# A transformer block with segment memory on one core: attention scheduled among the projections, V as the stationary operand, FFN in two token blocks

## Chip, cores, metric

One core of a Trainium2 chip. The metric is device time in microseconds (us) of one execution.

## The reference

One sequence of 2048 tokens, width 1024, bf16. A pre-norm block: attention in four segments with a compressive memory that is carried from segment to segment, then a gated FFN of width 3584. Cut to what is computed:

```python
def _A_ref(x, wq, wk, wv, wo, beta):            # x: layernorm of A_x, [1, 2048, 1024]
    q, k, v = x @ wq, x @ wk, x @ wv             # 32 heads of 32, 4 segments of 512 tokens
    phi = lambda t: where(t > 0, t + 1.0, exp(t))
    g = sigmoid(beta)                            # one gate a head
    M, z = 0, 0                                  # memory of a head: 32 x 32, and 32
    for s in range(4):
        p = softmax(qs @ ks.T * 32**-0.5 + causal mask)
        a_dot = p @ vs
        a_mem = (phi(qs) @ M) / (phi(qs) @ z + 1e-06)
        o = g * a_mem + (1.0 - g) * a_dot
        M, z = M + phi(ks).T @ vs, z + phi(ks).sum(l)
    return o @ wo
h  = A_x + _A_ref(layernorm(A_x), ...)
h2 = h + (silu(ln @ w1) * (ln @ w3)) @ w2        # ln = layernorm(h); F = 3584
```

In matmuls of 128 x 128 weights against 512 columns the dense part is 768 for q, k and v, 256 for the output projection, 1792 for w1 and w3 and 896 for w2: 3712 in all.

## The kernel before

Five phases run one after the other, with a wait of every engine for every other between them (`sync_all`). Inside each phase the order is written out by hand, and every engine executes its own instructions in that order.

**Phase AB** (`phase_AB`): the layer norm of 16 token tiles (statistics L317 and L320, square root on ACT L151, apply L324), transposes on PE (L343) and copies on ACT (L352), then per 512 tokens the projections (L383) on four PSUM banks, copied out by DVE (L392) and ACT (L395, L406). All of q, k (transposed, `qT`, `kT`) and v (`vaug`, with a 33rd column per head) stay in SBUF.

**Phase C** (`phase_C`): 8 groups of 4 heads, 4 segments each, so 32 steps, pipelined by one: the head of a step between the tail pieces of the step before. The head makes the scores of four key tiles (`head_kc`; L580, four matmuls side by side, one for each head's 32 rows), each followed by one exponential on ACT over four banks (L589) and the triangle mask on DVE (L603). The tail multiplies by V (L631): a 128 x 128 block of exponentials is the stationary operand and 33 columns of V move through, so 1280 matmuls of 33 columns in all; then it reads the memory (L677, 384 matmuls of 33 columns), divides and adds on DVE (L700 to L709), and updates the memory (L648 to L752). phi is computed for a whole group at a time (`group_prep`, L548 to L555).

**Phase D** (`phase_D`): per token tile, transposes of the attention output (L839), copies (L848, L853), the output projection (L869), residual add (L883), second layer norm (L896 to L903), transposes (L921) and copies (L928, L934).

**Phase F** (`phase_F`): 14 chunks of w1 and w3 (256 columns each), all 2048 tokens for each: gate (L1011), up (L1017), sigmoid on ACT (L1028), two products on DVE (L1033, L1038). **Phase G** (`phase_G`): four blocks of 512 tokens; w2 comes in 7 slices for every block (28 loads of 1 MB); the matmuls (L1098) fill eight banks, and at the end of a block eight residual adds (L1120) and eight stores follow.

## Time and profile before

| | |
|---|---|
| Time, median of 3 runs | 1230.05 us (1229.1 to 1231.36) |
| Span of the profiled execution | 1229.1 us; its own time is 1229.1 us too (the fastest of the three) |
| PE (matmul) busy | 981.4 us, 80% |
| DVE / ACT / POOL busy | 507.0 / 339.9 / 21.1 us |
| DMA traffic | 66.05 MB, mean 54 GB/s |

L1011 stands for line 1011 of the kernel. PE is TensorE, PEld its weight loads, DVE VectorE, ACT ScalarE, POOL GpSimd. PEclk is the granted clock of TensorE as a share of 2.4 GHz, so 0.50 is 1.2 GHz. A group's mean duration of a matmul contains its latency, and matmuls overlap: what one costs in a stream is read from the distance of the starts. An "idle before" names what ended an engine's wait.

### The profile page before, as it was taken

How to read it: one execution, taken by the hardware profiler on the slowest of the kernel's cores; microseconds unless marked ns; L12 is line 12 of the kernel's file. 1: busy time of each engine (PE TensorE's matmuls, PEld its weight loads, DVE VectorE, ACT ScalarE, POOL GpSimd, SP SyncE). 2: the span in 40 equal slices, each digit the busy share in tenths (PEclk: the TensorE clock that was granted, in tenths of full speed). 3: DMA queues.
4: the chain of work that ended last, by engine and by line, in shares of the span. 5: the costliest groups of instructions: out<-in, count | busy, mean ns of one | idle time of the engine just before them, and what ended most of it. 6: DMA issues, size and time to landing. Idle time of an engine off the chain costs nothing.

```text
span 1229.1 us, 16143 instructions
## 1 busy us (share of the span) xinstructions
PE 981.4 (80%) x6752; PEld 470.9 (38%) x6752; DVE 507.0 (41%) x1010; ACT 339.9 (28%) x423; POOL 21.1 (2%) x43
## 2 busy tenths in 40 slices
PE   4988989244444544578869999999999997999997
PEld 2434444132222322334424444444444443444443
DVE  5240310466666776657734333334444430101011
ACT  3224122565555665522211111111111110000000
POOL 1000000000000000000000000000000000001011
PEclk9999989555555555589989999999999998999999
DMA  8010000100000000011121111111111103555453
GB/s 307 1 35 1 1 1 1 69 2 1 1 1 1 2 1 1 1 44 52 43 69 35 36 35 35 35 53 50 35 36 35 35 1 107 176 164 201 139 189 120
DMA packets 54232, 66.05 MB, mean 54 GB/s; under 512 B 1936, under 2 KB 30608, under 8 KB 54160
## 3 DMA queue, kind: packets, MB, share of 16 engines
q1 hardware_dynamic: 52624, 60.83, 15.8%
q0 software_dynamic: 1536, 4.20, 0.9%
q8 instruction: 53, 0.87, 0.3%
q14 instruction: 19, 0.16, 0.0%
HBM read 60.83 MB, written 4.19 MB: 53 GB/s over the span
## 4 chain that ended last, share of the span: by engine, by line
PE 71%; ACT 16%; DVE 8%; DMA 2%; issue 2%; POOL 0%; SPq 0%; ACTq 0%; DVEq 0%; POOLq 0%
PE psall L1011 16%; PE psall L1017 16%; PE psall L1098 15%; PE psall L383 12%; ACT eTbuf L589 11%; PE psall L869 5%; PE psall L580 4%; ACT tmp L552 2%; ACT xnT L352 1%; DVE lnst L317 1%; DVE pkTg L555 1%; PE psall L631 1%; DMA w2b<-in_B_w_dram 1%; PE psall L921 1%; PE psall L648 1%
## 5 line engine op out<-in xcount | busy, mean ns | idle before, releaser
L1011 PE MATMUL psall<-hnT,w1b 128*128 128x512 bf16 x896 | 213.2, 381 | 6.8 <-DMA w3b<-in_B_w_dram 6.8
L1017 PE MATMUL psall<-hnT,w3b 128*128 128x512 bf16 x896 | 211.7, 379 | 0.0
L1098 PE MATMUL psall<-w2b,hmT 128*128 128x512 bf16 x896 | 195.3, 381 | 7.7 <-DMA w2b<-in_B_w_dram 7.7
L589 ACT ACTIVATE eTbuf<-psall 128x2048 bf16<-128x2048 f32 (+3 forms) x128 | 158.4, 1237 | 70.6 <-PE psall L580 69.9
L580 PE MATMUL psall<-qT,kT 32*128 32x256 bf16 (+3 forms) x512 | 58.0, 443 | 148.4 <-ACT eTbuf L589 142.8
L1033 DVE TENSOR_TENSOR sg<-sg,psall 128x512 bf16<-128x512 bf16 x112 | 77.1, 688 | 238.5 <-PE psall L1017 226.6
L1028 ACT ACTIVATE sg<-psall 128x512 bf16<-128x512 f32 x112 | 66.9, 597 | 315.6 <-PE psall L1011 315.6
L1098 PEld LDWEIGHTS psall<-w2b,hmT 128*128 128x128 bf16 x896 | 87.9, 98 | 115.2 <-issue 10.0
L1011 PEld LDWEIGHTS psall<-hnT,w1b 128*128 128x128 bf16 x896 | 87.9, 98 | 113.4 <-issue 8.6
L1017 PEld LDWEIGHTS psall<-hnT,w3b 128*128 128x128 bf16 x896 | 87.7, 98 | 105.9 <-issue 0.5
L1120 DVE TENSOR_TENSOR ob<-hnat,psall 128x512 bf16<-128x512 bf16 x32 | 22.0, 688 | 180.3 <-PE psall L1098 180.0
L1038 DVE TENSOR_TENSOR hmT<-sg,psall 128x512 bf16<-128x512 bf16 x112 | 76.9, 687 | 3.8
L580 PEld LDWEIGHTS psall<-qT,kT 32*128 32x128 bf16 x512 | 14.0, 99 | 164.2 <-ACT eTbuf L589 159.5
L869 PE MATMUL psall<-wosb,otT 128*128 128x512 bf16 x256 | 60.1, 389 | 16.0 <-ACT otT L853 16.0
L631 PE MATMUL psall<-vaug,eTbuf 128*128 128x33 bf16 x1280 | 53.8, 193 | 23.9 <-DVE onat L709 22.0
L383 PE MATMUL psall<-xnT,wq 128*128 128x512 bf16 x256 | 64.7, 418 | 9.3 <-ACT xnT L352 6.8
L603 DVE TENSOR_TENSOR eTbuf<-eTbuf,triu 128x512 bf16<-128x512 bf16 x128 | 54.4, 425 | 40.6 <-ACT eTbuf L589 30.4
L631 PEld LDWEIGHTS psall<-vaug,eTbuf 128*128 128x128 bf16 x1280 | 43.5, 107 | 56.3 <-DVE onat L709 33.2
L383 PE MATMUL psall<-xnT,wk 128*128 128x512 bf16 x256 | 55.9, 379 | 0.0
L383 PE MATMUL psall<-wv,xnT 128*128 128x512 bf16 x256 | 55.9, 379 | 0.0
L383 PEld LDWEIGHTS psall<-xnT,wq 128*128 128x128 bf16 x256 | 26.5, 105 | 46.4 <-issue 11.1
L392 DVE CAST qT<-psall 128x512 bf16<-128x512 f32 x32 | 21.3, 689 | 54.1 <-PE psall L383 54.1
(70 smaller groups left out, 596.0 us busy)
## 6 DMA issues: line engine op xcount, KB each, us to landing
w2b<-in_B_w_dram SPq DMA_DIRECT2D x28, 1024.0 KB, 5.3
w1b<-in_B_w_dram SPq DMA_DIRECT2D x14, 512.0 KB, 4.0
w3b<-in_B_w_dram SPq DMA_DIRECT2D x14, 512.0 KB, 5.4
xb<-in_A_x_dram SPq DMA_DIRECT2D x4, 1024.0 KB, 6.8
xr<-in_A_x_dram SPq DMA_DIRECT2D x16, 256.0 KB, 2.7
out_dram<-ob POOLq DMA_DIRECT2D x32, 128.0 KB, 2.4
wq<-in_A_wq_dram SPq DMA_DIRECT2D x1, 2048.0 KB, 12.8
wk<-in_A_wk_dram SPq DMA_DIRECT2D x1, 2048.0 KB, 17.7
```

The lines of the kernel that those rows point to most:

```text
L383: o = pe.matmul(self.bank(b), lhsT, rhs, start=(c == 0), stop=(c == NKC - 1))
L580: o = pe.matmul(self.bank(j, N), lhsT, rhs, start=True, stop=True, tile_position=(32 * j, 0))
L589: o = act.activation(eTbuf[:, :, offs[kc]:offs[kc] + N], src, AF.Exp, scale=scale)
L603: o = dve.tensor_tensor(eTbuf[:, :, offs[kc]:offs[kc] + 128], eTbuf[:, :, offs[kc]:offs[kc] + 128], self.triu[:, :].unsqueeze(1).to_broadc ...
L631: o = pe.matmul(self.ps_all[:, ucol(j, i):ucol(j, i) + 33], lhsT, rhs, start=(kc == 0), stop=(kc == i))
L869: o = pe.matmul(self.bank(bb + half), ob[:, c, :], self.wo_sb[:, c, half * 512:(half + 1) * 512], start=(c == 0), stop=(c == NKC - 1))
L1011: o = pe.matmul(self.bank(bg), w1b[i][:, c, jj * 128:(jj + 1) * 128], self.hnT[:, c, tc * 512:(tc + 1) * 512], start=(c == 0), stop=(c == ...
L1017: o = pe.matmul(self.bank(bu), w3b[i][:, c, jj * 128:(jj + 1) * 128], self.hnT[:, c, tc * 512:(tc + 1) * 512], start=(c == 0), stop=(c == ...
L1028: o = act.activation(sg[si][:, :], self.bank(bg), AF.Sigmoid)
L1033: o = dve.tensor_tensor(sg[si][:, :], sg[si][:, :], self.bank(bg), op=ALU.mult)
L1038: o = dve.tensor_tensor(self.hmT[:, fc, tc * 512:(tc + 1) * 512], sg[si][:, :], self.bank(bu), op=ALU.mult)
L1098: o = pe.matmul(self.bank(bb), self.hmT[:, fc, t * 128:(t + 1) * 128], w2b[k % 2][:, jj, half * 512:(half + 1) * 512], start=(fc == 0), st ...
```

## The change

The kernel is rewritten. All work is entered into a graph as operations with the engines that may run them, a cost in ns, a class (lower goes first), and the buffers they read and write. `schedule` then plays the graph through: whenever an engine is free it takes the ready operation of the lowest class whose PSUM banks are free, and its cost decides when its users become ready. The order that comes out for each engine is fixed in the program; on the chip an engine executes its list in that order, with semaphore waits. The costs are linear in the columns (`mm_ns`: n/2.4 + 2.6 ns for a matmul, `dve_ns`: 150 + n/0.96, `act_ns`: 185 + 0.834 n, `pool_ns`: 220 + 1.05 n), with a fixed latency to the user (260 ns behind PE, 110 to 130 behind the others) and 60 ns for a change of the PE's tiling.

What is computed by what:

- **Segments instead of phases.** Layer norm, q, k, v and memory of segment s+1 are entered ahead of the attention of segment s and share the engines with it, as does the output projection of the segment (`run`, below). Classes on PE: scores 0, PV 1, memory read 2, transposes of the norms 2 and 3, memory update 4, output projection 5, projections 6, FFN up 7, FFN down 8. wq, wk and wv come in halves of 1 MB, anew for every segment, into three buffers. q, k and v have two buffers each (even and odd segments).
- **PSUM.** Attention has banks 0 to 3 (scores), 4 and 5; everything dense has banks 6 and 7; only once the last score operation has started does the FFN get the other six as well.
- **Scores.** Three exponentials a step instead of four (the third and fourth key tile share one of 384 columns a head); the mask is an `affine_select` on POOL, 4 a step, instead of a product on DVE.
- **PV.** V (128 keys x 32) is the stationary operand, the exponentials move through, 512 to 128 columns, four heads side by side in column tiles; the output is transposed, so the transposes of phase D go. The row sums come from a second such pass with a matrix of one column of ones (`ones32`). The memory is read by two full matmuls a step. Division: 32 x 32 block transposes on DVE of the sums, a reciprocal, and block transposes that spread it again; the memory part is multiplied and added on POOL.
- **phi** is taken on 1024 columns at a time: exponential on ACT, minimum and maximum on DVE, the sum on POOL. The norm's square root is a power of -0.5 on POOL, the FFN's sigmoid a Tanh with the rest in DVE's products.
- **FFN.** Two blocks of 1024 tokens. `ffn_up` loads w1 and w3 in 14 chunks for each block (so twice in all); `ffn_down` keeps all 7 MB of w2 resident, works one half of a token tile after the other (28 matmuls into one bank), adds the residual, which was written to and read back from a DRAM scratch (`h_scr`), and stores. The buffer `hm` of the FFN's first block lies over q, k and v (its first 12 of 28 tiles over those of the even segments), w1 and w3 over the projections' weights and the normed input, w2 over attention buffers.
- All transfers are issued from the SP queue, in the planned order.

The core of the diff, new lines only (the old kernel goes entirely):

```diff
+    PAGE = 1024
+    LAT = {"pe": 260.0, "act": 110.0, "dve": 110.0, "pool": 130.0, "dma": 150.0}
+    SWITCH = 60.0
+    DMA_RATE = 260.0
+    DMA_FIX = 1900.0
...
+            moved = True
+            while moved:
+                moved = False
+                for e in ENGINES:
+                    if not free[e]:
+                        continue
+                    skipped = []
+                    pick = None
+                    while avail[e]:
+                        item = heapq.heappop(avail[e])
+                        o = item[2]
+                        if o in started:
+                            continue
+                        if not can_start(o):
+                            skipped.append(item)
+                            continue
+                        pick = o
+                        break
+                    for it in skipped:
+                        heapq.heappush(avail[e], it)
...
+def act_ns(n, ptr=0):
+    return 185.0 + n * 0.834 + 93.0 * ptr
+def dve_ns(n, mode=1):
+    return 150.0 + n / (0.96 * mode)
+def pool_ns(n):
+    return 220.0 + n * 1.05
+def mm_ns(n):
+    return max(n, 66) / 2.4 + 2.6
...
+    def dense_group(self, late=False):
+        g = Group([(6,), (7,)],
+                  ("att", [(4,), (5,), (0,), (1,), (2,), (3,)]) if late else None, True)
+        return g
...
+    def ln(self, k, src, dst, cls):
...
+        ve, rs = self.lnve[:, k:k + 1], self.rstd[:, k:k + 1]
+        var, mean = self.lnmv[:, k, 1:2], self.lnmv[:, k, 0:1]
+        mh = self.mhalf[:, :]
+        self.pool_op(lambda e: e.tensor_scalar(ve, var, self.EPS, None, op0=ALU.add), 1,
+                     [var], [ve], 0)
+        self.pool_op(lambda e: e.tensor_tensor(rs, ve, mh, op=ALU.pow), 300, [ve, mh], [rs], 0)
+        self.dve_op(lambda e: e.tensor_scalar(dst, src, mean, rs, op0=ALU.subtract,
+                                              op1=ALU.mult), 540.0, [src, mean, rs], [dst], cls)
...
+    def phi(self, src, dst, cls):
...
+        self.act(e_, src, AF.Exp, act_ns(1024), cls=cls)
+        self.dve_op(lambda e: e.tensor_scalar(e_, e_, 1.0, None, op0=ALU.min), dve_ns(1024, 4),
+                    [e_], [e_], cls)
+        self.dve_op(lambda e: e.tensor_scalar(r, src, 0.0, None, op0=ALU.max), dve_ns(1024, 4),
+                    [src], [r], cls)
+        self.pool_op(lambda e: e.tensor_tensor(dst, e_, r, op=ALU.add), 1024, [e_, r], [dst],
+                     cls)
...
+    def unit(self, s, g, q, k, v, pq):
+        G = self.g
+        u = self.n_unit % 2
+        self.n_unit += 1
+        e0, e1, e2 = self.e0[u], self.e1[u], self.e2[u]
+        pm = (s - 1) % 2
...
+        for batch in (0, 1, 2):
+            gr = self.queue(0, 1, 2, 3)
+            kcs = ((0,), (1,), (2, 3))[batch]
+            width = (512, 384, 384)[batch]
+            et = (e0, e1, e2)[batch]
+            def emit(e, gr, kcs=kcs):
+                ins = []
+                off = 0
+                for kc in kcs:
+                    n = 512 - 128 * kc
+                    for j in range(4):
+                        r = slice(32 * j, 32 * j + 32)
+                        ins.append(e.matmul(self.bank(gr, j, n, off),
+                                            k[r, g, 128 * kc:128 * kc + 128],
+                                            q[r, g, 128 * kc:512], start=True, stop=True,
+                                            tile_position=(32 * j, 0)))
+                    off += n
+                return ins
+            o = G.op("pe", 60 + width / 2.4, emit, reads=[k[:, g, :], q[:, g, :]], cls=0,
+                     group=gr, gate="att")
+            o.mode = "row"
+            def ex(e, gr, et=et, width=width):
+                b = gr.banks[0]
+                src = self.ps[:, b * 512:(b + 4) * 512].rearrange(
+                    "p (j n) -> p j n", j=4)[:, :, 0:width]
+                return [e.activation(et[:, :, :], src, AF.Exp, scale=self.scale)]
+            G.op("act", act_ns(4 * width), ex, writes=[et[:, :, :]], cls=0, group=gr)
+            for c in (0,) if batch < 2 else (0, 256):
+                m = et[:, :, c:c + 128]
+                self.pool_op(lambda e, m=m: e.affine_select(
+                    m, m, pattern=[[0, 4], [1, 128]], compare_op=ALU.is_ge, fill=0.0, base=0,
+                    channel_multiplier=-1), 512, [m], [m], 1)
...
+        gm = self.queue(4) if s else None
+        gn, gd = self.queue(4), self.queue(5)
+        if s:
+            Mb, zs = self.Mbf[pm][:, g, :], self.zsel[pm][:, g, :]
+            self.mms(gm, [(lambda gr: self.bank(gr), Mb, pq, True, True, 512)], 2)
+            gcol = self.gcol[:, g:g + 1]
+            Nm = self.Nm[:, :]
+            G.op("act", act_ns(512, 1), lambda e, gr: [e.activation(
+                Nm, self.bank(gr), AF.Copy, scale=gcol)], reads=[gcol], writes=[Nm], cls=1,
+                group=gm)
+            self.mms(gd, [(lambda gr: self.bank(gr), zs, pq, True, True, 512)], 2)
+        for gr, what in ((gn, "n"), (gd, "d")):
+            for kc, src in pieces():
+                def emit(e, gr, kc=kc, src=src, what=what):
+                    ins = []
+                    b = gr.banks[0]
+                    for j in range(4):
+                        r = slice(32 * j, 32 * j + 32)
+                        lhsT = v[:, kc, g, r] if what == "n" else self.ones32[:, :]
+                        first = kc == 0 and (what == "n" or s == 0)
+                        ins.append(e.matmul(
+                            self.ps[r, b * 512 + 128 * kc:(b + 1) * 512], lhsT, src[:, j, :],
+                            start=first, stop=True, tile_position=(0, 32 * j),
+                            skip_group_check=True))
+                    return ins
+                reads = [src, v[:, kc, g, 0:128] if what == "n" else self.ones32[:, :]]
+                o = G.op("pe", 60 + (512 - 128 * kc) / 2.4, emit, reads=reads, cls=1, group=gr)
+                o.mode = "col"
...
+        def spread(dst, col):
+            src = Rc[:, :, col:col + 1].to_broadcast([128, 16, 32])
+            self.dve_op(lambda e: e.transpose(dst, src), dve_ns(512), [rc], [dst], 0)
+        spread(R0, 0)
+        oT = self.oT[s % 2][:, g, :]
+        dst = o1 if s else oT
+        G.op("dve", dve_ns(512), lambda e, gr: [e.scalar_tensor_tensor(
+            dst, self.bank(gr), ocol, R0, op0=ALU.mult, op1=ALU.mult)], reads=[ocol, R0],
+            writes=[dst], cls=0, group=gn)
+        if s:
+            spread(R1, 1)
+            Nm = self.Nm[:, :]
+            self.pool_op(lambda e: e.tensor_tensor(o2, Nm, R1, op=ALU.mult), 512, [Nm, R1],
+                         [o2], 2)
+            self.pool_op(lambda e: e.tensor_tensor(oT, o1, o2, op=ALU.add), 512, [o1, o2],
+                         [oT], 2)
...
+                    dst = self.hm[fc][:, tc * 512:(tc + 1) * 512]
+                    self.g.op("dve", dve_ns(512), lambda e, gr, t1=t1, dst=dst: [
+                        e.scalar_tensor_tensor(dst, t1, 0.5, self.bank(gr), op0=ALU.mult,
+                                               op1=ALU.mult)], reads=[t1], writes=[dst], cls=2,
+                        group=gu)
...
+        self.ln1(0)
+        self.qkv(0)
+        self.g.dma(self.wo[:, :, :], self.A_wo.rearrange("(c p) n -> p c n", p=128), cls=3)
+        for s in range(4):
+            if s < 3:
+                self.ln1(s + 1)
+                self.qkv(s + 1)
+                self.memory(s)
+            self.attention(s)
+            self.wo_stage(s)
+        for blk in range(2):
+            self.ffn_up(blk)
+            self.ffn_down(blk)
+        self.g.schedule()
...
```

## Rows read from the trace of the kernel before

**Rows 1.** Busy time by stretch: length, PE, PEld, DVE, ACT, POOL, granted clock, DMA share, GB/s.
```profile
0.00:31.00 31.00, 13.40 (x64) 6.74 (x64) 17.87 (x41) 9.61 (x20) 3.62 (x11) 1.00 0.85 305
...
31.00:216.00 185.00, 172.29 (x834) 78.51 (x832) 38.44 (x72) 53.16 (x96) 0.00 (x0) 0.96 0.02 6
...
222.00:515.00 293.00, 129.42 (x2542) 79.25 (x2543) 194.17 (x468) 179.91 (x142) 0.00 (x0) 0.50 0.01 4
...
515.00:620.00 105.00, 81.16 (x620) 42.23 (x616) 73.72 (x156) 25.84 (x49) 0.00 (x0) 0.92 0.14 41
...
620.00:1020.00 400.00, 389.18 (x1800) 176.12 (x1800) 156.45 (x231) 69.05 (x115) 0.00 (x0) 0.99 0.14 37
...
1020.00:1229.00 209.00, 195.34 (x896) 87.88 (x896) 23.19 (x34) 0.00 (x0) 17.43 (x32) 0.97 0.48 161
```

**Rows 2.** The page's chain that ended last, share of the span by engine.
```profile
PE 71%; ACT 16%; DVE 8%; DMA 2%; issue 2%; POOL 0%; SPq 0%; ACTq 0%; DVEq 0%; POOLq 0%
```

**Rows 3.** The chain in order of time, FFN: start, length, what.
```profile
639.83 1.73 PE psall L1011 x8
...
657.09 1.73 PE psall L1011 x8
```

**Rows 4.** Timeline of one attention step: start, length, engine, line, form, [idle before].
```profile
251.39 0.51 PE L580 MATMUL psall<-qT,kT 32*128 32x384 bf16 x4 [9.69 <-ACT eTbuf L589]
...
251.83 0.52 PE L631 MATMUL psall<-vaug,eTbuf 128*128 128x33 bf16 x12
...
251.95 1.45 ACT L589 ACTIVATE eTbuf<-psall 128x1536 bf16<-128x1536 f32 x1 [0.61 <-PE psall L580]
...
255.45 0.34 PE L730 MATMUL psall<-vaug,pknat 128*32 128x33 bf16 x16
```

**Rows 5.** Start of the projections, timeline.
```profile
21.69 9.59 PE L383 MATMUL psall<-xnT,wq 128*128 128x512 bf16 x32 [1.30 <-ACT xnT L352]
...
31.43 7.08 PE L383 MATMUL psall<-xnT,wq 128*128 128x512 bf16 x32 [0.15 <-DVE qT L392]
```

**Rows 6.** Stage D, timeline: output projection and transposes of two tiles.
```profile
540.37 3.61 PE L869 MATMUL psall<-wosb,otT 128*128 128x512 bf16 x16 [1.02 <-ACT otT L853]
...
544.01 0.62 PE L921 MATMUL psall<-ident,hn 128*128 128x128 bf16 x8
...
544.47 0.61 PE L839 MATMUL psall<-ident,onat 128*128 128x128 bf16 x8
...
546.10 3.61 PE L869 MATMUL psall<-wosb,otT 128*128 128x512 bf16 x16 [1.02 <-ACT otT L853]
```

**Rows 7.** Groups by line and form, ACT and DVE: count, busy us, mean ns, idle before.
```profile
L589 ACT ACTIVATE eTbuf<-psall 128x2048 bf16<-128x2048 f32 x32 | 60.1, 1877 | 18.0 <-PE psall L580 17.3
...
L589 ACT ACTIVATE eTbuf<-psall 128x1536 bf16<-128x1536 f32 x32 | 46.4, 1451 | 19.6 <-PE psall L580 19.6
...
L392 DVE CAST qT<-psall 128x512 bf16<-128x512 f32 x32 | 21.3, 689 | 54.1 <-PE psall L383 54.1
...
L317 DVE BATCH_NORM_STATS2 lnst<-xb 128x6 f32<-128x512 bf16 x32 | 20.6, 685 | 7.7 <-DMA xb<-in_A_x_dram 7.0
...
L324 DVE TENSOR_SCALAR xb<-xb,lnmv,rstd 128x1024 bf16<-128x1024 bf16 x16 | 8.8, 547 | 0.6
...
L552 ACT ACTIVATE tmp<-tmp 128x1536 bf16<-128x1536 bf16 x16 | 23.7, 1482 | 43.2 <-DVE tmp L548 43.2
...
L700 DVE RECIPROCAL rrs<-psall 128x32 f32<-128x32 f32 x24 | 8.6, 358 | 7.2 <-PE psall L677 5.2 <-PE psall L580 0.5
```

**Rows 8.** The same view, POOL.
```profile
L298 POOL MEMSET vaug<- 128x512 bf16 x1 | 2.3, 2313 | 0.0
...
L205 POOL TENSOR_SCALAR_AFFINE_SELECT triu<-triu 128x128 bf16<-128x128 bf16 x1 | 0.3, 292 | 0.1
...
L209 POOL MEMSET epscol<- 128x1 f32 x1 | 0.1, 98 | 0.0
```

**Rows 9.** The page's DMA issues: KB each, median us to landing.
```profile
xr<-in_A_x_dram SPq DMA_DIRECT2D x16, 256.0 KB, 2.7
```

More of the change, by code (lines that the diff above doesn't have):

```diff
@@ L1 @@
+import heapq
 from contextlib import ExitStack
@@ new lines, with __init__ @@
+SIZE = {F32: 4, BF16: 2}
+ENGINES = ("pe", "act", "dve", "pool", "sp")
+class Op:
+    __slots__ = ("engs", "eng", "cost", "emit", "deps", "users", "cls", "seq", "missing",
+                 "ready", "start", "end", "pos", "signal", "tok", "group", "first", "last",
+                 "mode", "bytes", "kind", "snap", "gate")
+    def __init__(self, engs, cost, emit, cls, seq):
+        self.engs, self.cost, self.emit, self.cls, self.seq = engs, cost, emit, cls, seq
+        self.eng = None
+        self.deps, self.users = {}, []
+        self.missing = 0
+        self.ready = 0.0
+        self.start = self.end = None
+        self.pos = None
+        self.signal = False
+        self.tok = None
+        self.group = None
+        self.first = self.last = False
+        self.mode = None
+        self.bytes = 0
+        self.kind = None
+        self.snap = None
+        self.gate = None
@@ L1133, in bass_sequential_preLN__memory_aug_infini_attn__glu_gated_swiglu__prompt_kernel, with build @@
+            self.g.emit()
+def build(nc, A_x, A_wq, A_wk, A_wv, A_wo, A_beta, B_x, B_w1, B_w3, B_w2, out):
+    with ExitStack() as es:
+        k = Kernel(nc, es, A_x, A_wq, A_wk, A_wv, A_wo, A_beta, B_w1, B_w3, B_w2, out)
+        k.run()
+    return k
 def bass_sequential_preLN__memory_aug_infini_attn__glu_gated_swiglu__prompt_kernel(
```

1686 lines of the change are left out of this document (657 added, 1029 removed).

## Prediction

> **What bounds the kernel now.** Read the busy time by stretch first [rows 1]. In the projections (31 to 216 us), F (620 to 1020) and G (1020 to 1229) PE is busy for 93 to 97% at a granted clock of 0.96 to 0.99, the level of 2.4 GHz. In the attention (222 to 515) no engine is full: PE 44%, DVE 66%, ACT 61%, and the clock stands at 0.50, 1.2 GHz, behind a PE that pauses after every few matmuls. The first 31 us hold 13 us of PE work, D (515 to 620) 81 us in 105. The chain that ended last says the same by engine: PE 71%, ACT 16%, DVE 8% [rows 2]. So the kernel is a PE kernel with about 430 us in which PE waits for others or runs at half clock, 293 of them the attention. In the timeline of a step, scores of 384 columns end, the exponential takes 1.45 us, and PE, idle 9.69 us ahead of these scores, waits for ACT [rows 4].
>
> **The price of a matmul.** In F eight matmuls of 512 columns follow each other every 1.726 us (ten such groups in 17.26 us [rows 3]), 0.2158 us each, 0.42 ns a column. Eight transposes take 0.46 us, from 544.01 to 544.47 [rows 6], 0.0575 each.
>
> **PE's work after the change, at full clock.** Dense, unchanged in number: 3712 x 0.2158 = 801.0 us. Transposes: 256 for the two norms and 96 for phi(k), 352 x 0.0575 = 20.2; the 128 of the attention output and the 1280 matmuls of 33 columns with their weight loads go. Memory update: 96 of 129 columns, at the transposes' price 5.5. Memory read: 24 steps x 2 x 0.2158 = 10.4. Scores: 32 steps of 1280 columns with four heads side by side: 0.54 us a step, 17.3. That row tiles do run side by side is in the trace: four of 384 columns take 0.51 us at 1.2 GHz [rows 4], where 4 x 0.32 would be 1.28 in series. PV: numerators and sums, twice 1280 columns a step, 34.5 us if column tiles run side by side too. The nearest row is the memory update, 16 matmuls in column tiles with 16 weight loads in 0.34 us at 1.2 GHz [rows 4]; in series 16 x 33 columns alone take 0.44. I take side by side; in series PV is 138 us. Changing tiles: behind the scores of 384 columns (0.32 us at 1.2 GHz) the next kind starts after 0.44 us [rows 4], 0.12 lost. There are 11 tiled batches a step, 352 in all; I take 0.06 each at the full clock, 21.1, and 0.12, 42.2, as the other end. Sum: 801.0 + 20.2 + 5.5 + 10.4 + 17.3 + 34.5 + 21.1 = 910 us.
>
> The Trainium skill, TensorE: Matmul & The Clock Gate, Part 3, gives 2.38 times for three column tiles instead of 3. By it, as an estimate, PV would cost 43.5 us and the sum below would be 11 us more; the row above can't tell the two apart.
>
> **Start and tail.** The first projection starts at 21.69 us now [rows 5]. After: a tile of 256 KB lands in 2.7 us [rows 9]; its norm takes 2 x 0.685 + 0.547 on DVE and smaller pieces, about 2.9; only two tiles fit, so the third is loaded behind the first one's transposes. 1 + 2.7 + 2.9 + 0.6 + 2.7 + 2.9 + 2.3 + 1.5 = 16.6 us, of which 15 are not in the 910 (10 to 20 as ends). The first 32 matmuls after a pause took 9.59 us where the next 32 took 7.08 [rows 5]: 2.5. Tail: one residual add (0.69) and one store (at most the 2.7 of a 256 KB load), about 4 us, where G ends with eight adds and eight stores. G's stretch is 209 us for 896 x 0.2158 = 193.4 [rows 1], and these 16 us go, the waits for w2 with them. Floor: 910 + 15 + 2.5 + 4 = 931.5.
>
> **What PE loses in the mixed stretch.** Outside it lie the first segment's projections (192, 41.4 us) and the FFN's part that runs alone. FFN can start under the last segment's attention with the 12 of 28 tiles whose buffers lie over the even segments: 384 matmuls, 83 us. It leaves 2304, 497.2 us. Mixed: 910 - 41.4 - 497.2 = 371 us of PE work, with the attention's chain inside. Two rows show what PE gets done when it takes turns with DVE and ACT. In the projections 736 matmuls and 96 transposes (164.4 us) took 185 us, 89%, cold clock after each pause included [rows 1]. In D a tile's 16 matmuls and 16 transposes (4.37 us) took 5.73, 76%, from 540.37 to 546.10 [rows 6], with nothing else to run in the gaps. The new order has dense work for the gaps, but also two dense banks instead of four, more handoffs, and a fixed order that stalls whenever a planned cost was too low. I take 85%, nearer to the projections: 371 / 0.85 = 437, a loss of 66. Ends: 46 at 89% and 117 at 76% (145 with the higher price of tile changes). Below nothing it can't go, since PE's work is counted at full clock.
>
> **Do the others keep up?** A middle segment has PE work of 85 us, so 100 at 85%. ACT: exponentials 8 x (1.877 + 2 x 1.451) = 38 [rows 7], phi 8 x about 1.05 (1.482 for 1536 columns), the memory's copy 8 x 0.69, and a share of the copies out of PSUM of 13: 65 us. DVE: a step has four passes of 512 f32 at 0.69 and two small ones of at most 0.36 [rows 7], 28 us; norms of eight tiles 18, residuals and half the projections' copies 14, the rest at most 22: 82 us. Neither ends last, but DVE is near. POOL, nearly unused now, gets the mask: selects (32 of 512 elements), memory combination (16 of 512), phi sums (8 of 1024) and small ones: 33.8 thousand elements a lane and some 8.5 us of fixed costs at 0.1. From the select of 128 elements in 0.292 us and a single one in 0.098 the price is 1.5 ns an element; the strided memset of 512 in 2.313 gives 4.5 [rows 8]. That is 59 to 161 us. I take the select's row, as the largest part is the same operation: covered by PE.
>
> The Trainium skill, GPSIMD Engine Reference, section 3, speaks against this part: it calls the engine the wrong choice for ordinary elementwise work, with 4497 ns for an add of 2048. By that figure the two-input part, as an estimate, costs 2.2 ns an element and POOL 71 us a segment; the sum stays, and the POOL rival below would be unlikelier than I set it. No run here shows a two-input operation on POOL.
>
> **DMA.** w1 and w3 come twice, wq, wk and wv four times, h goes out and back, w2 once instead of four times. F moves its chunks at a DMA share of 0.14, G at 0.48 [rows 1]; twice F's share is 0.28, hidden under the matmuls. SP issues everything in one list, so a store that waits holds the loads behind it; with two chunks of weights in hand (27 us of PE) I cost that at nothing, and at one uncovered chunk, some 6 us, if the cover is gone.
>
> **Sum.** 931.5 + 66 = 997 us against the profiled execution, whose span and time are both 1229.1; the median is 1 us above it, so 998.
>
> **The rivals.**
> - *The list holds* (25%): PE gets over 89% in the mixed stretch, 932 to 977. For it: in a middle segment every other engine has a fifth of slack. Against: two banks, so each copy must be prompt.
> - *POOL ends last* (17%): at 4.5 ns an element the four segments cost 103, 161, 161 and 135, 560 us. With 17.5 + 20 us ahead of the first step, 16 for the last output projection, 497 and 4 behind it: about 1115. It decides from 2.7 ns an element (100 us a middle segment). For it: in-place selects and two inputs are not in the trace. Against: the select's row.
> - *Column tiles in series* (5%): 103 us more PE work, 121 at 85%: about 1118. Against it the 0.34 us of 16.
> - *The order doesn't interleave* (3%): attention runs by itself. A step's chain is 4.8 us of exponentials and three handoffs with scores of about 0.7, 7 us, 224 for 32; less its 85 us of PE work that is 139 more than the floor, 1071.
> - *The clock stays down* (5%, slower than before): PE's list stops at the head of a waiting attention operation with dense matmuls behind it, as in the attention now, where 44% busy goes with 0.50. At 1.2 GHz the mixed 371 us become 742, in all 1303 at best. It decides when the stretch passes 371 + 1229 - 931.5 = 669 us, a PE share at full clock below 56%. Against it: D had 0.92 at 77% busy [rows 1], and dense work at half clock fills the gaps itself.
>
> **How the numbers follow.** The forecast, 977 to 1077 around 998, has 45%; the rivals the rest. The range 945 to 1115 leaves out the lower third of the second case and the upper part of POOL, column tiles and the clock, some 2 in 10. Its own range and all cases but the last are faster by far more than 0.2%, which is about what a measurement can tell from no change: 94% faster, 1% same, 5% slower.
>
> **What would show it.** PE busy of 85% or more, granted clock over 0.9, between 60 and 480 us; dense groups of eight still 1.73 us apart; four column tiles of 512 columns in 0.25 to 0.4 us at full clock; selects near 0.87 us; POOL under 75% in the middle segments; the FFN's first gate matmuls under the last attention; 2304 matmuls alone in about 500 us; some 4 us behind the last matmul. Wrong would be: PE's largest idle times ended by POOL, a clock of 0.5 over tens of us, or waits for w1 or w3.

## The result, and the profile after

The changed kernel takes 1023.16 us (median of 4 runs, 1022.1 to 1027.14) against 1230.6 for the kernel before beside it: a ratio of 0.8324, 95% interval 0.8307 to 0.8342. The prediction was 998, range 945 to 1115. The profiled execution has a span of 1022.1 us, which the prediction put at 997: 25 us more.

From the page of the changed kernel: busy time by engine, the granted clock in 40 slices, and the chain that ended last by engine (it answers to [rows 2]).

```profile
PE 947.3 (93%) x5639; PEld 419.5 (41%) x5744; DVE 418.9 (41%) x710; ACT 320.6 (31%) x353; POOL 235.2 (23%) x317
...
PEclk9999899899997999999999999999999999999999
...
PE 78%; POOL 7%; DVE 7%; ACT 2%; DMA 2%; issue 2%; SPq 1%; DVEq 0%; ACTq 0%; POOLq 0%
```

PE is busy for 93% of the span instead of 80%, the attention's hole with a clock of 0.50 is gone, and POOL has appeared in the chain. Busy time by stretch of the changed kernel (columns as in [rows 1]):

```profile
0.00:31.00 31.00, 4.12 (x32) 3.09 (x32) 9.14 (x28) 6.20 (x9) 6.76 (x25) 1.00 0.67 221
31.00:150.00 119.00, 109.91 (x855) 47.32 (x870) 62.31 (x116) 65.51 (x59) 45.10 (x72) 0.97 0.30 98
150.00:188.00 38.00, 33.90 (x248) 16.05 (x250) 11.14 (x24) 20.34 (x24) 17.69 (x19) 1.00 0.37 125
188.00:210.00 22.00, 13.70 (x168) 5.64 (x167) 20.56 (x37) 16.37 (x15) 20.18 (x30) 0.77 0.12 36
210.00:292.00 82.00, 76.40 (x539) 32.34 (x549) 45.30 (x78) 45.82 (x46) 44.73 (x53) 1.00 0.28 91
292.00:322.00 30.00, 19.14 (x241) 8.79 (x241) 23.46 (x41) 22.54 (x20) 26.54 (x31) 0.79 0.16 53
322.00:440.00 118.00, 113.73 (x916) 43.06 (x933) 65.18 (x119) 75.44 (x73) 71.11 (x83) 0.99 0.28 86
440.00:1000.00 560.00, 557.26 (x2568) 254.77 (x2618) 179.04 (x268) 68.35 (x112) 3.12 (x8) 1.00 0.26 75
```

Three things are to be seen. Up to 31 us PE has done 4 us. From 31 to 440 us it is busy for 367 of 409 us, and the longest pauses stand in two places: 188 to 210 and 292 to 322, where PE is busy for 62 to 64%, DVE for 78 to 93%, POOL for 88 to 92%, and the clock falls below 0.8. From 440 us on, the FFN alone, PE is busy for 557 of 560 us. A shorter pause of the same kind is hidden in the row of 31 to 150 us, and the largest single item of PE's 42 idle us between 31 and 440 us is waiting for POOL's masks (us in total, times, longest):

```profile
100.00:115.00 15.00, 10.66 (x136) 5.08 (x134) 10.52 (x23) 10.19 (x8) 9.45 (x20) 0.77 0.32 109
```

```profile
PE ps L814 <- POOL eC L783: 10.0, 7, 3.3
```

**The start.** Timeline of the changed kernel's first 42 us (start, length, engine, line, form, [idle before]); SPq is the time in which SP issues transfers:

```profile
1.70 0.43 SPq L176 DMA_DIRECT2D wp<-in_A_wq_dram  x1
...
2.79 3.80 SPq L176 DMA_DIRECT2D wp<-in_A_wv_dram  x1
...
10.62 0.43 SPq L176 DMA_DIRECT2D wo<-in_A_wo_dram  x1
11.17 19.04 SPq L176 DMA_DIRECT2D xs<-in_A_x_dram  x4
...
22.91 1.88 DVE L628 BATCH_NORM_STATS2 lnst<-xs 128x6 f32<-128x512 bf16 x3 [4.59 <-DMA xs<-in_A_x_dram]
...
26.58 1.01 PE L549 MATMUL ps<-ident,xs 128*128 128x128 bf16 x8 [16.14 <-DVE xs L637]
...
31.07 11.29 PE L537 MATMUL ps<-xnT,wp 128*128 128x512 bf16 x38 [1.27 <-ACT xnT L560]
```

The third x tile waits in SP's list behind the weights: wq at 1.70, wk, then wv at 2.79, whose issue alone lasts 3.80 us, and wo (2 MB) at 10.62. It lands at 22.9 us, PE stands still for 16.14 us until it is normed, and the first projection starts at 31.07 instead of the 16.6 I had worked out ([rows 5] has 21.69).

**The price of a change of tiling.** PE's timeline in the first attention, at full clock:

```profile
61.98 1.04 PE L537 MATMUL ps<-xnT,wp 128*128 128x512 bf16 x4
62.95 0.24 PE L814 MATMUL ps<-eC,v 128*32 128x128 bf16 x4
...
63.79 0.24 PE L814 MATMUL ps<-eC,ones 128*32 128x128 bf16 x4
63.96 1.04 PE L537 MATMUL ps<-xnT,wp 128*128 128x512 bf16 x4
...
64.93 0.34 PE L763 MATMUL ps<-qT,kT 32*128 32x384 bf16 x4
65.20 0.40 PE L814 MATMUL ps<-eA,v 128*32 128x512 bf16 x4
65.43 0.39 PE L814 MATMUL ps<-eA,ones 128*32 128x512 bf16 x4
```

Four dense matmuls take 0.863 us at 0.2158 each, but the next kind starts 0.97 us after them; scores of 384 columns take 0.16 and are followed after 0.27. Column tiles of 128 columns take 0.05 and are followed by dense matmuls after 0.17. So a change costs 0.107, 0.11 and 0.12 us in these rows, each way about the same. Over all changes of the stretch that no wait hides it is mostly 0.09 to 0.11 us; the 0.105 of the text below lies in the upper part of that. Between the two PV groups, which share a tiling, nothing is lost: four column tiles of 512 columns in 0.23 us. Counted through the timeline, PE changes its tiling 394 times between 30 and 440 us.

**POOL and DVE.** Groups by line and form (count, busy us, mean ns | idle before):

```profile
L783 POOL TENSOR_SCALAR_AFFINE_SELECT eC<-eC 128x512 bf16<-128x512 bf16 x64 | 41.9, 655 | 21.6 <-ACT eC L778 20.5
L850 POOL TENSOR_TENSOR o<-Nm,R1b 128x512 f32<-128x512 f32 x24 | 30.8, 1283 | 10.2 <-DVE R1b L839 10.0
...
L686 POOL TENSOR_TENSOR pk<-phe,phr 128x1024 bf16<-128x1024 bf16 x12 | 25.4, 2120 | 31.0 <-DVE phe L682 28.7 <-DVE T L829 2.3
...
L829 DVE TENSOR_SCALAR T<-T 128x16 f32<-128x16 f32 x24 | 8.9, 370 | 0.3
```

A select of 512 elements costs 0.65 us (I had 0.87), a two-input operation of 512 costs 1.28 and one of 1024 costs 2.12 (I had 0.87 and 1.64). The last row is an addition of a constant to 16 columns, with a mean of 370 ns. The timeline of the dry stretch shows why:

```profile
190.70 1.27 POOL L852 TENSOR_TENSOR oT<-o,o 128x512 bf16<-128x512 f32 x1
...
190.74 1.27 DVE L829 TENSOR_SCALAR T<-T 128x16 f32<-128x16 f32 x1
...
191.92 2.12 POOL L686 TENSOR_TENSOR pq<-phe,phr 128x1024 bf16<-128x1024 bf16 x1
...
195.47 0.35 PE L814 MATMUL ps<-eC,ones 128*32 128x256 bf16 x8 [3.26 <-POOL eC L783]
```

The DVE operation on 16 columns starts beside a two-input POOL operation and ends with it, 1.27 us; with no POOL operation beside it, it takes 0.16 to 0.18. Two things go further than that. A mask's select holds it too: here the operation starts inside the select and ends with it, after 0.57 us.

```profile
362.08 0.64 POOL L783 TENSOR_SCALAR_AFFINE_SELECT eB<-eB 128x512 bf16<-128x512 bf16 x1 [2.33 <-ACT eB L778]
362.18 0.57 DVE L829 TENSOR_SCALAR T<-T 128x16 f32<-128x16 f32 x1
```

And not every DVE operation is held: the reciprocal that follows runs beside the phi sum of 191.92 us and takes its usual time (its mean is 0.345).

```profile
192.52 0.33 DVE L833 RECIPROCAL Rc<-T 128x32 f32<-128x32 f32 x1
```

In the timeline above, PE then waits 3.26 us for a select that stands behind a phi sum on POOL.

### The profile page after: what moved, and what is told of

It is laid out like the page before. It is cut to its first block, busy times and chain, and to the rows that moved or that the text cites. A ratio compares the mean times of both kernels' runs of the same rounds, so it can differ in the third digit from the quotient of the medians.

```text
span 1022.1 us, 13535 instructions
## 1 busy us (share of the span) xinstructions
PE 947.3 (93%) x5639; PEld 419.5 (41%) x5744; DVE 418.9 (41%) x710; ACT 320.6 (31%) x353; POOL 235.2 (23%) x317
## 4 chain that ended last, share of the span: by engine, by line
PE 78%; POOL 7%; DVE 7%; ACT 2%; DMA 2%; issue 2%; SPq 1%; DVEq 0%; ACTq 0%; POOLq 0%
PE ps L537 72%; PE ps L814 3%; POOL pk L686 2%; POOL pq L686 2%; PE ps L763 2%; DMA xs<-in_A_x_dram 1%; SPq L176 1%; PE ps L549 1%; DVE h L868 1%; POOL oT L852 1%; POOL eC L783 1%; DVE phe L682 1%; POOL o L850 1%; DVE phr L684 1%; ACT phe L512 1%
## 5 line engine op out<-in xcount | busy, mean ns | idle before, releaser
L537 PE MATMUL ps<-hnT,w1b 128*128 128x512 bf16 x879 | 221.9, 379 | 2.4 <-DMA w1b<-in_B_w_dram 1.4
L537 PE MATMUL ps<-hnT,w3b 128*128 128x512 bf16 x875 | 221.2, 379 | 1.1
L898 ACT ACTIVATE sg<-ps 128x512 bf16<-128x512 f32 x112 | 66.9, 597 | 420.7 <-PE ps L537 420.7
L537 PE MATMUL ps<-w2b,hm 128*128 128x512 bf16 x877 | 195.2, 379 | 1.0
L901 DVE SCALAR_TENSOR_TENSOR t<-sg,ps 128x512 bf16<-128x512 bf16 x112 | 76.9, 687 | 224.2 <-ACT sg L898 224.2
L537 PEld LDWEIGHTS ps<-w2b,hm 128*128 128x128 bf16 x896 | 87.7, 98 | 105.7
L537 PEld LDWEIGHTS ps<-hnT,w1b 128*128 128x128 bf16 x896 | 87.2, 98 | 106.1 <-issue 5.1
L537 PEld LDWEIGHTS ps<-hnT,w3b 128*128 128x128 bf16 x896 | 87.1, 98 | 104.9 <-issue 0.9
L537 PE MATMUL ps<-xnT,wp 128*128 128x512 bf16 x492 | 122.3, 390 | 6.1 <-ACT xnT L560 3.4
L906 DVE SCALAR_TENSOR_TENSOR hm<-t,ps 128x512 bf16<-128x512 bf16 x112 | 76.8, 686 | 34.9 <-PE ps L537 31.8
```

Source lines behind the costliest of these rows:

```text
L537: return [e.matmul(p[0](gr), p[1], p[2], start=p[3], stop=p[4]) for p in part]
L898: self.g.op("act", act_ns(512), lambda e, gr, sg=sg: [e.activation(sg, self.bank(gr), AF.Tanh, scale=0.5)], writes=[sg], cls=2, group=gg)
L901: e.scalar_tensor_tensor(t1, sg, 1.0, self.bank(gr), op0=ALU.add, op1=ALU.mult)], reads=[sg], writes=[t1], cls=2,
L906: e.scalar_tensor_tensor(dst, t1, 0.5, self.bank(gr), op0=ALU.mult, op1=ALU.mult)], reads=[t1], writes=[dst], cls=2,
```

## The experiments

Times are medians; the kernel before took 1230.1 to 1231.05 beside each. Line numbers of an experiment can differ by a few from those of the changed kernel. Every edit is planned anew, so the order of the whole list changes with it. A new order alone was worth 9 us in one run below, so a difference of a few us in the time can't be put down to an edit by itself; the stretches of the trace have to bear it out.

### The start: x tiles ahead of the weights

```diff
-            x = self.xs[t % 2][:, :]
+            xb = (self.xs + self.h)[t] if s == 0 else self.xs[t % 2]
+            x = xb[:, :]
...
```

> Edit: in the first segment the third and fourth token tile are loaded into two other buffers (h), so that all four x loads stand ahead of the weights in SP's list; nothing else changes. Theory (the late start is the queue: the third x tile lands at 22.9 us because it is issued behind 3 MB of q, k, v weights and 2 MB of wo): the first projection starts at 15 to 18 us instead of 31.07 and the time falls by 11 to 16 us, to 1007 to 1012. Rival (the start is bound by the weights or by the norm's chain): the first projection stays later than 25 us and the time falls by less than 5 us.

1008.78 us, 14.4 less than the changed kernel. The first projection, in PE's timeline of this run:

```profile
16.65 3.57 PE L537 MATMUL ps<-xnT,wp 128*128 128x512 bf16 x8 [1.26 <-ACT xnT L560]
```

It starts at 16.65 us, so the late start was the third tile's late load. The edit lifts two things at once, the tile's place behind the weights and its wait for a buffer. The trace of the changed kernel puts most of it on the weights: the buffer is free at 8.29 us, when the first transposes end, SP comes to the load at 11.17, and it lands 11.7 us later, where the first tile's load took 2.7.

### Without the masks

```diff
-            for c in (0,) if batch < 2 else (0, 256):
+            for c in ():
                 m = et[:, :, c:c + 128]
```

> Edit: the 128 affine_select masks on POOL are left out (the attention is then not causal within the diagonal blocks); everything else stays, and the list is planned anew. It takes 83 us of POOL's 235. Theory P (in the stretches where the projections have run dry, 190 to 210 and 290 to 330 us, POOL sets the pace of the attention): those stretches shorten, PE's waits for POOL eC go, and the time falls by 10 to 25 us, to 997 to 1012. Rival (POOL is covered everywhere, PE loses its time to changes of tiling): the time stays within 4 us of 1022.

1010.89 us, 12.3 less. The two dry stretches in this run:

```profile
188.00:210.00 22.00, 16.39 (x180) 7.07 (x183) 21.00 (x34) 16.61 (x15) 16.62 (x18) 0.77 0.09 25
292.00:322.00 30.00, 22.14 (x259) 9.38 (x261) 25.72 (x44) 23.44 (x21) 20.66 (x21) 0.89 0.04 10
```

PE is busy for 16.4 and 22.1 us instead of 13.7 and 19.1, and POOL is down to 17 of 22; but DVE is now busy for 21 of 22. Some 3 us of the gain are something else by the price above: PE changes its tiling 364 times instead of 394. POOL does pace the dry stretches, but DVE stands right behind it. Whether the selects cost their own time on POOL or the time for which they hold DVE, this run can't tell: both go.

### The planner told what operations cost

```diff
-    SWITCH = 60.0
+    SWITCH = 105.0
...
-                    channel_multiplier=-1), 512, [m], [m], 1)
+                    channel_multiplier=-1), 512, [m], [m], 1, 640.0)
...
-                         [o2], 2)
+                         [o2], 2, 1270.0)
```

> Edit: only the planner's costs are changed, to durations measured in the trace of the changed kernel: two-input POOL operations of 512 and 1024 elements 1270 and 2120 ns (were 758 and 1295), selects 640 (758), power 570 (300), memory product 600, 310 for the small ones; a change of tiling 105 ns each way (was 120 into a tile and 60 back). The operations are the same, their order is not. Theory M (the fixed order stalls because POOL was planned too fast): PE's waits in the mixed stretch, some 42 us, fall by a third to a half, time 1000 to 1012. Rival (waits come from a lack of dense work and from port sharing, which no order mends): within 5 us of 1022.

1013.9 us, 9.3 less: short of the theory's range by 2 us, and beyond the rival's. PE's idle time from 31 to 440 us falls from 42.2 to 31.7, a quarter; the dry stretches stay (PE 16.8 of 22 and 23.5 of 30). A better order is worth 9 us here and doesn't make dense work appear where there is none.

### Attention by itself

```diff
                 self.memory(s)
+            self.g.stage()
             self.attention(s)
+            self.g.stage()
             self.wo_stage(s)
```

`stage()` makes everything entered later wait for everything entered before.

> Edit: the attention of each segment waits for everything entered before it, and everything behind it waits for the attention, so nothing dense runs among the steps; all else (V-stationary PV, FFN) stays. My prediction's price for this rival was 1071 from a floor of 932; with the start of 31 us and tile changes at 0.105 us it is 1071 + 14 + 20 = 1105. Theory (interleaving is what brings most of the gain): 1085 to 1150, the granted clock at 0.50 in the attention, a step every 7 to 8 us. Rival (the reshaped attention and the FFN bring the gain, interleaving little): below 1050.

1211.63 us: 188.5 more than the changed kernel, and far more than I gave it. Stretches of this run (attention of the first segment, the dense work behind it, attention of the second):

```profile
138.00:193.00 55.00, 33.19 (x369) 9.93 (x368) 17.03 (x28) 38.83 (x25) 19.71 (x31) 0.52 0.00 1
193.00:280.00 87.00, 69.50 (x393) 34.60 (x400) 29.83 (x58) 28.42 (x38) 21.30 (x34) 0.89 0.34 109
280.00:343.00 63.00, 34.90 (x368) 10.67 (x376) 27.40 (x50) 46.16 (x36) 43.14 (x47) 0.59 0.00 1
```

The attention takes about what the price said, 55 to 64 us a segment, 245 in all instead of 224, at a clock of 0.52 to 0.59. What the price left out is the other side: the dense stretches between 31 and 536 us last 324 us (107, 87, 93 and 37) for some 230 us of PE work (an estimate from the prediction's prices). Norms, phi of the memory and loads make pauses of their own there, some 94 us with the lowered clock behind them, and in the changed kernel the attention's work lies beside these.

Part of the 94 us is the experiment's own. The edit holds back transfers as well, which its text doesn't say: nothing is loaded under the attention (a DMA share of 0.00), and the next weights, and the residual for the output projection, are asked for only when it has ended.

```profile
197.30 0.37 SPq L188 DMA_DIRECT2D wp<-in_A_wq_dram  x1
...
210.16 1.89 PE L561 MATMUL ps<-ident,pk 128*128 128x128 bf16 x16 [6.95 <-DVE h L880]
```

Here PE waits 6.95 us for a residual add that waits for its load, and 7.5 us in the next segment. So 188 us is an upper bound for what interleaving is worth; attention by itself with its loads ahead wasn't run.

### Fewer changes of tiling

```diff
-            yield 0, e0[:, :, :]
-            yield 1, e1[:, :, :]
-            yield 2, e2[:, :, 0:256]
-            yield 3, e2[:, :, 256:384]
+            yield (0, e0[:, :, :]), (1, e1[:, :, :])
+            yield (2, e2[:, :, 0:256]), (3, e2[:, :, 256:384])
...
```

> Edit: the eight PV operations of a step on PE become four (first and second key tile together, third and fourth together, for numerators and for sums); the same matmuls. In the changed kernel PE changes its tiling 394 times, each at 0.105 us at full clock. Theory S (these changes are the term I sized too low, and PE is what ends last): changes fall to 250 to 320 and the time by 0.105 us for each, 8 to 15 us, to 1007 to 1014. Rival (PE's changes lie in waits for POOL and ACT anyway, and pieces that start later make the chain of a step longer): 1019 or more.

1015.64 us, 7.5 less, with 310 changes instead of 394. 84 x 0.105 is 8.8, so the price about holds; the time ends 1.6 us above the theory's range and below the rival's. What takes the last microsecond is not shown, and it is within the spread of the runs (1013.3 to 1017.3).

### A second buffer for the normed input

```diff
-            out = self.xnT[:, :, i * 128:(i + 1) * 128]
+            out = (self.hnT[1] if s == 1 else self.xnT)[:, :, i * 128:(i + 1) * 128]
...
+        xnT = self.hnT[1] if s == 1 else self.xnT
...
```

> Edit: the normed, transposed input of the second segment lies in a buffer of its own (hnT1, free until that segment's output projection), so that of the third segment can be written while the projections of the second still run. Theory D (the pauses come where dense work runs dry, and at 188 to 210 us it is dry because the input has one buffer): the stretch at 188 to 210, PE 12 of 20 us and clock 0.74, fills up, and the time falls by 5 to 10 us; the like stretch at 292 to 322, which this edit leaves alone, stays. Rival (the norm's DVE and POOL work, not the buffer, is late): within 3 us of 1022.

1010.38 us, 12.8 less, more than expected, though the changes of tiling rise to 422. The same two stretches:

```profile
188.00:210.00 22.00, 20.06 (x184) 7.67 (x183) 14.96 (x24) 15.59 (x15) 17.45 (x17) 1.00 0.15 49
292.00:322.00 30.00, 23.51 (x205) 9.01 (x210) 18.60 (x34) 19.42 (x17) 22.48 (x31) 0.77 0.04 10
```

The first is filled (20.1 of 22 us, clock 1.00), the second, which the edit leaves alone, is not. So the first dry stretch was made by one buffer: the third segment's input could not be written while the second one's projections read it. The edit opens one more place than its text names. The second segment's input can now be written while the first one's projections read theirs, and the pause that the changed kernel has from 100 to 115 us (PE busy for 10.66 us, clock 0.77) is filled as well:

```profile
100.00:115.00 15.00, 14.01 (x179) 6.56 (x184) 10.50 (x21) 11.51 (x11) 8.87 (x18) 1.00 0.34 113
```

That may be why the gain is larger than expected.

### The combination of memory and attention on DVE

```diff
-            self.pool_op(lambda e: e.tensor_tensor(o2, Nm, R1, op=ALU.mult), 512, [Nm, R1],
-                         [o2], 2)
+            self.dve_op(lambda e: e.tensor_tensor(o2, Nm, R1, op=ALU.mult), dve_ns(512),
+                        [Nm, R1], [o2], 1)
...
```

> Edit: the product and the sum that combine memory and local attention (24 steps x 2, 1.28 us each on POOL) go to DVE, at a planned 0.68 us each. POOL loses 61 us, DVE gains 33. Theory P (POOL and what it holds up on DVE, where an operation of 16 columns takes 1.27 us beside a two-input POOL operation and 0.18 without, set the pace of the dry stretches): the mean of DVE L829 falls from 370 to below 220 ns, the time by 6 to 15 us. Rival (DVE, near 80% in a middle segment by my working, becomes the bound): the time rises.

1024.99 us, 1.8 more, which lies inside the spread of the changed kernel's own runs (1022.1 to 1027.14): the theory's gain of 6 to 15 us is not there, and the rise that the rival forecast isn't shown either. The first dry stretch, and in the timeline one DVE operation of 16 columns with the POOL operation beside it:

```profile
188.00:210.00 22.00, 13.08 (x156) 4.73 (x163) 21.26 (x40) 17.38 (x15) 12.64 (x17) 0.80 0.04 13
```

```profile
187.90 2.58 POOL L686 TENSOR_TENSOR pq<-phe,phr 128x1024 bf16<-128x1024 bf16 x1 [0.71 <-PE ps L537]
...
188.41 2.11 DVE L829 TENSOR_SCALAR T<-T 128x16 f32<-128x16 f32 x1
```

POOL has time to spare now (12.6 of 22 us), DVE none (21.3). And the constant's addition got slower, a mean of 467 ns: it now runs beside the phi sums and ends with them, and these are twice as long as the operations that went. My theory that POOL alone sets the pace falls; in this stretch the two engines are full together, and moving these two operations from one to the other gains nothing.

### Three edits, and what still adds to them

> Edit: the early x loads of the first run, the measured planner costs of the third and the second input buffer together. If the three mend different stretches their gains add, 14 + 9 + 5 to 10: 990 to 994. If the better order already fills the stretch that the buffer opens, 997 to 1001. Either way the first projection starts at 16.7 us.

984.92 us, 38.2 less than the changed kernel; 14.4 + 9.3 + 12.8 are 36.5, so they add. (The diffs are those above.)

> Edit: the three edits of e8_three (984.9 us, 404 changes of tiling) and the merged PV operations. Theory S: the changes fall by some 80 to 90 and the time by 0.105 us for each, to 974 to 979. Rival (with the dry stretches filled the waits for exponentials count, and larger pieces make the step's chain longer): 982 or more.

980.57 us, 4.3 less than with three, for 69 changes fewer (404 to 335), which at 0.105 would be 7.2. That is between theory and rival: PE has a new wait of 5.8 us for one norm.

The next run leaves the merged PV out again and changes phi on top of the three edits:

```diff
-        self.dve_op(lambda e: e.tensor_scalar(r, src, 0.0, None, op0=ALU.max), dve_ns(1024, 4),
-                    [src], [r], cls)
-        self.pool_op(lambda e: e.tensor_tensor(dst, e_, r, op=ALU.add), 1024, [e_, r], [dst],
-                     cls)
+        self.dve_op(lambda e: e.scalar_tensor_tensor(dst, src, 0.0, e_, op0=ALU.max, op1=ALU.add),
+                    dve_ns(1024), [src, e_], [dst], cls)
```

> Edit: the three edits of e8_three, and phi's maximum (DVE) and sum (POOL, 24 x 2.12 us) become one scalar_tensor_tensor on DVE of 1024 columns, planned at 1.22 us instead of 0.42. POOL loses 51 us, DVE gains some 14, and a DVE tensor_scalar no longer stands behind a phi sum on the shared port. Theory (two-input POOL work holds DVE up, 1 to 2 us at a time): the mean of DVE L831 falls from 654 to below 400 ns and the time by 3 to 10 us, to 975 to 982. Rival (DVE is what the full stretches lack, as when the combination went to DVE): 984 or more.

972.45 us, 12.5 less than with three, and the best of all: 0.7897 of the kernel before (0.7882 to 0.7911). The stretch that stays dry lies from 260 to 280 us in these runs, since all of it starts earlier. That stretch, and all from 16 to 440 us, with three edits and then with this one:

```profile
260.00:280.00 20.00, 12.87 (x141) 5.58 (x132) 18.11 (x32) 12.97 (x11) 16.74 (x24) 0.74 0.11 42
16.00:440.00 424.00, 396.85 (x3149) 169.22 (x3206) 260.14 (x452) 253.19 (x247) 229.47 (x292) 0.98 0.35 111
```

```profile
260.00:280.00 20.00, 16.48 (x189) 7.04 (x189) 18.90 (x34) 14.35 (x12) 18.40 (x28) 1.00 0.14 41
16.00:440.00 424.00, 406.45 (x3210) 173.68 (x3267) 275.88 (x469) 251.00 (x242) 190.39 (x268) 1.00 0.37 116
```

The constant's addition, with three edits and then with this one:

```profile
L831 DVE TENSOR_SCALAR T<-T 128x16 f32<-128x16 f32 x24 | 15.7, 654 | 0.4
```

```profile
L829 DVE TENSOR_SCALAR T<-T 128x16 f32<-128x16 f32 x24 | 8.5, 353 | 0.3
```

PE is busy for 16.5 us in the dry stretch instead of 12.9, at a clock of 1.00 instead of 0.74, and for 406 of 424 us instead of 397. Unlike the move of the combination, this takes 39 us off POOL for 16 more on DVE, and takes away the longest operations that hold DVE up. Which of the two brings the gain, no run separates.

> Edit: all five edits together: early x loads, measured planner costs, a second input buffer, merged PV operations, phi's maximum and sum in one DVE operation. If the gain of the merged PV (4.3 us on top of three edits) and that of phi (12.5 us) add: 966 to 970. If they mend the same waits: 971 to 975.

974.55 us: the gains of the merged PV and of phi don't add. With 341 changes of tiling instead of 411 it isn't faster than without the merged PV. In the stretch that stays dry PE is busy for as long (16.5 us), but at a lower clock, 0.76 instead of 1.00, and with fewer matmuls, 153 instead of 189:

```profile
260.00:280.00 20.00, 16.45 (x153) 6.70 (x153) 18.93 (x36) 15.11 (x13) 17.25 (x30) 0.76 0.12 37
```

The time lies in the range that I gave for the case that the two mend the same waits; that they do is not shown.

## Why the prediction was right, and where its terms were off

The span was 1022.1 us for a forecast of 997. By the steps of the sum:

- **Dense matmuls, 0.2158 us each:** right. In the chain that ended last the FFN stands in rows of 49 matmuls and 10.74 us, which is 48 starts 0.2158 apart and the 0.38 us that one lasts, and from 440 to 1000 us PE has 3 us idle.

```profile
448.52 10.74 PE ps L537 x49
```

- **Column tiles side by side:** right, 512 columns four times in 0.23 us, 3.75 times one after the other (0.863). The Trainium skill, TensorE: Matmul & The Clock Gate, Part 3, has 2.38 times for three tiles; by it I had 9 us more PE work. The measurement decides: side by side is worth nearly all of its four.
- **Changes of tiling:** mis-sized. 352 x 0.06 = 21 us in the sum; some 394 at 0.105 are 41, 20 us more, which is my upper end. I halved the 0.12 us seen at 1.2 GHz [rows 4] for the full clock; it hardly shrinks. The merged PV bears it out: 84 changes fewer, 7.5 us less, 0.09 each.
- **Start:** mis-sized. 16.6 us to the first projection, measured 31.07: 14.5 more. The step priced each load by itself and said of SP's one list only that a store could hold loads behind it; the list's first entries, 5 MB of weights ahead of a 256 KB tile, were to be had from the classes (x loads need a free buffer, weights don't) and were not looked at. The early x loads give back 14.4 us. That this run starts at 16.65 us, on my 16.6, is partly luck: my sum has the third tile wait for a buffer, and the run does away with that wait too.
- **Loss in the mixed stretch:** about right as a sum. PE's work is 910 + 20 = 930; less that, the 29 us of idle start and 3 of tail, the span leaves 60 us, where I had 66 and 2.5. Idle PE is 42 of it, the lowered clock most of the rest (0.96 over 409 us). As a share, PE's 324 us of work there (371 less the 67 of FFN that did not come in, and 20 more) took 384, or 84% where I had 85%. The working was not right, so the agreement is luck in its make-up: it spread the loss evenly. Most stretches run at 89 to 96%, two at 62 to 64%. The first of these was made by the single input buffer, as the second buffer showed, and while it is dry POOL and DVE are both near full (20.2 and 20.6 of 22 us), so that relieving POOL alone left DVE at 21 (the runs without masks and with the combination on DVE). That the second has the like cause is only argued: no run gave it a buffer. What speaks for it is its time: the fourth segment's input is written from 295 to 319 us, and its projections begin at 320.
- **Do the others keep up?** Right that neither ends last as a mean, wrong as a method. From 230 to 330 us POOL is busy for 60.6 us where I had 59, DVE for 61.5 where I had 82; both were weighed over a segment in which dense work is always at hand. Where it runs dry, both are at 78 to 93%. One of my signs of being wrong came true there: PE's two longest waits between 31 and 440 us, 3.3 us each, end with POOL, and the waits for its masks are 10 of 42 us. The operations' price was too low for two inputs: the Trainium skill, GPSIMD Engine Reference, section 3, gave 2.2 ns an element as an estimate, and 1.28 us for 512 and 2.12 for 1024 (2.5 and 2.1 ns an element) agree with it better than my 1.5 from the select's row.
- **FFN under the last attention:** wrong, 71 matmuls instead of 384 by 440 us, since that attention still had projections beside it. It moves no PE work, so the sum didn't see it.
- **The rivals:** the attention apart costs 1211.6, not 1071. The price took the dense stages as free of pauses; they have some 94 us of them. So interleaving is up to 188 of the 207 us, since that run held back its loads too, and the reshaped attention and FFN gave at least 19 without it. Of the others, POOL's price came out between the select's row and the strided memset's, 1.3 ns an element for selects and 2.1 to 2.5 for two inputs, short of the 2.7 from which POOL would have ended last as a mean; but it did so in the dry stretches. The clock stayed at 0.96, and the list lost 16% where its own rival had at most 11.

The sum came out 25 us short: 14.5 of start, 20 of changes, and 9 too much for losses and 1 for the tail. Two terms in the same direction were mis-sized, and a loss set too high took 9 us back. What carried it was counting PE's work and two rows that bound its losses.

## What to carry to other kernels

In a kernel that one engine bounds, count that engine's work at full rate, price each change of mode by a pair of starts at the clock that will hold, and ask of every other engine not its mean share but its share where the bounding engine's filler work runs out. Look for the one buffer that keeps the next stage's input from being written: here a second one was worth 12.8 us, a better order 9.3. And read the list of a shared issue queue from its first entry: here weights that no buffer held back went ahead of the tile that PE needed first, and that cost 14 us.

## What the runs showed of the hardware

- A DVE `tensor_scalar` of 16 columns from SBUF to SBUF, 0.18 us alone, that starts inside a POOL operation lasts until that one ends: 1.27 us beside a two-input one of 1.27, 2.11 beside a phi sum, 0.57 beside a select. The norm's `tensor_scalar` of 0.55 us takes up to 2.33. A reciprocal beside a phi sum took its usual 0.33, so it is not all of DVE that stands. The Trainium skill, SBUF — State Buffer, section SBUF: two separate sides, says that the pair of ports which the two engines share is locked for a whole instruction by the one that starts first, and that the other fully blocks, where the DVE operation is in a mode that uses two ports or has two inputs from SBUF; these rows agree, but no row says which mode an operation was in.
- A change of PE's tiling costs 0.09 to 0.11 us at 2.4 GHz, little less than the 0.12 of the one pair read at 1.2 GHz [rows 4].
- A power of -0.5 of one element a lane takes 0.57 us on POOL, where a multiplication of 512 elements takes 1.28.
